# Four edits around the hand-over from MoE 1 to MoE 2: the queue that stores x's parts, the first part loads, the logits' steps and the Sinkhorn steps

## The chip, the cores and the metric

The kernel runs on one core of one Trainium2 chip. The metric is the device time of one execution in microseconds (us); lower is better. Three runs of the kernel before give a median of 2110.19 us (2109.23 to 2112.42).

## The reference, cut to what matters

```python
def reference(**kwargs):
    attn_out = _attn_ref(...)                    # B=4, H=8, S=576, D=64, causal attention plus a memory term
    x = attn_out.transpose(0, 2, 1, 3).reshape(2304, 512)
    x = (silu(x @ w_gate) * (x @ w_val)) @ w_out # MoE 1: 512 -> 1536 -> 512
    logits = x @ w_gate2                         # MoE 2: 8 experts, 512 -> 1024 -> 512
    P = np.exp(logits - logits.max())
    for _ in range(8):                           # Sinkhorn
        P /= P.sum(1, keepdims=True) + 1e-09
        P /= P.sum(0, keepdims=True) + 1e-09
        P *= N / E
    for e in range(E):
        out += P[:, e:e + 1] * (np.maximum(x @ w1[e], 0.0) @ w2[e])
```

## The kernel before, in words

Everything is computed in pairs of rounded halves: a value is cast to a high part, the rest is subtracted out as a low part, and three products (high by high, high by low, low by high) make one matrix product on TensorE. ScalarE (ACT) makes most of the casts, VectorE (DVE) most of the subtractions.

The tile framework fixes the order of each engine's instructions when the program is built, by a time model of its own; on the chip each engine takes its instructions strictly in that order. `keep_in_program_order` pins an instruction behind all that were traced before it on its engine; `issue_after(mark)` queues a block's instructions behind a mark on the mark's engine (in `behind`, the marks are the last load of a part, the last copy on ScalarE, and so on).

**x and its parts.** MoE 1 leaves x in one SBUF tile, `xacc`. MoE 2 uses a seven-product scheme on two by two blocks, so each pair of 256-token blocks of x is needed as seven parts (`B11`, `T1`, `T2`, `B21`, `T3`, `T4`, `B22`), each 512 KB as a pair of halves. `parts` (L731) and `parts_of` (L704) make them: a cast on ScalarE into a tile of `xl`, which has two buffers (L717); in the next step the subtraction on VectorE (L720); in the step after it a store to DRAM, issued on SyncE (SP, L723). The cast two parts later needs the same `xl` buffer, so it waits until that store has landed. Pairs 0 and 1 are made in MoE 1's third stage (14 stores), pair 2 in its last stage (7), pair 3 and the last 256 tokens in the first two pairs of MoE 2 (9): 30 stores. All loads of the kernel are issued on the same SP queue.

**MoE 2.** It goes over 16 units (half an expert each) and, in each, over four pairs of blocks and a rest. `unit_hidden` (L1257) makes a pair's hidden values in seven steps "H", of 12 matmuls each (L1270), every one with one part of x, read back from DRAM into a tile `xr` (four buffers, L1484). The function `right` keeps three part loads ahead of the one in use. The first four are issued before the loop, and their memory is that of the tiles of x that MoE 1's last matmuls "p" (L546) read. Chains of H steps sum into one PSUM bank `pc`, which ScalarE copies out between two of them (`keep`, L1277). Steps "O" make the output: `first_out` in unit 0 (L546, `pq`, copied to the sum by VectorE, L1410), `unit_out` after it (L1433, L1439). The output sum takes the memory of x, so L1410 cannot write before the last reader of x is done.

**Beside unit 0** run two generators, advanced by `behind` as the H and O steps go on: `last_parts` (every second step) and `routing` (every step). `routing` makes the logits of the last two chunks (`logits`, L672, with `two` set: tokens 1536 to 2047, m = 4, and 2048 to 2303, m = 2) and then the Sinkhorn iteration (`sinkhorn`, L1094). Each `yield` ends a step. The logits take 3 yields for each of 4 blocks and 2 more; in each block there is a cast (L681), a yield, a subtraction (L683), two yields and then the matmuls (L688). A Sinkhorn iteration takes five VectorE operations (L1112 to L1116), a yield, a matmul with ones (L1119), a yield and four VectorE operations (L1121 to L1124). The tiles `h` of the hidden values are in the pool `hc`, with eight buffers (`split_h`, L1242).

Of the kernel before, what the change touches and what calls it, by code (L numbers as in the profile page):

```python
# [9 lines left out]
F32R = mybir.dt.float32r  # L10
# [4 lines left out]
ALU = mybir.AluOpType  # L15
# [4 lines left out]
P = 128  # L20
B, H, S, D = 4, 8, 576, 64
NP = H // 2
NT = B * S
# [4 lines left out]
E = 8  # L28
# [104 lines left out]
def f32(ap):  # L133
    return ap.bitcast(F32)
# [21 lines left out]
def placed(pool, name, by):  # L156

    return pool.tile([P, 2 * 512 + 64], F32R, name=name)[:, by:by + 2 * 512].rearrange("p (a n) -> p a n", a=2)


class Kernel:
# [508 lines left out]
    def logits(self, psum, name, pool, first, last, two=None):  # L670

        nc, m = self.nc, last - first  # L672
        pl = psum.tile([P, 512], F32, name=name)
        for k in range(NK):
            src = self.x[:, k, first * P:last * P]
            if two:
                t = [pool.tile([P, 512], F32R, name=two)[:, 0:m * P] for _ in range(2)]
            else:
                t = pool.tile([P, 2, 512], F32R, name="xl")
                t = [t[:, a, 0:m * P] for a in range(2)]  # L680
            nc.scalar.copy(t[0], src)  # L681
            yield
            nc.vector.tensor_sub(t[1], src, f32(t[0]))  # L683
            yield
            if two:
                yield
            for a in range(2):
                nc.tensor.matmul(  # L688
                    pl[0:2 * E, 0:m * P], self.wgs[:, k], t[a], start=k + a == 0, stop=k == NK - 1 and a == 1
                )  # L690
        lt = pool.tile([P, 512], F32, name=two) if two else f32(pool.tile([P, 2, 512], F32R, name="xl")[:, 0])
        lt = lt[0:2 * E]
        nc.vector.tensor_copy(lt[:, 0:m * P], pl[0:2 * E, 0:m * P])
        yield
        yield
        pl = psum.tile([P, 512], F32, name=name)
        for t in range(m):
            nc.tensor.transpose(pl[:, t * 2 * E:(t + 1) * 2 * E], lt[:, t * P:(t + 1) * P], self.ident[0:2 * E, 0:2 * E])
        sums = self.Pw[:, first:last]
        pl = pl[:, 0:m * 2 * E].rearrange("p (t a e) -> p t a e", a=2, e=E)  # L700
        nc.vector.tensor_copy(sums, pl[:, :, 0])
        nc.vector.tensor_add(sums, sums, pl[:, :, 1])

    def parts_of(self, todo):  # L704


        nc, rest = self.nc, []
        for src, dst in [*todo, (None, None), (None, None)]:
            nxt = []
            for what in rest:  # L710
                nxt += what()
            rest = nxt
            if src is not None:
                src = src()
                t = self.xl.tile([P, 2, 512], F32R, name="xl")
                hi, lo = (t[:, n].rearrange("p (k t) -> p k t", k=2) for n in range(2))
                nc.scalar.copy(hi, src)  # L717

                def low(src=src, dst=dst, t=t, hi=hi, lo=lo):
                    nc.vector.tensor_sub(lo, src, f32(hi))  # L720

                    def store():
                        nc.sync.dma_start(dst, f32(t))  # L723
                        return []

                    return [store]

                rest.append(low)
            yield

    def parts(self, pair):  # L731

        t0, to = 2 * HT * pair, self.xparts[pair]
        q = {
            f"B{k + 1}{t + 1}": self.x[:, 2 * k:2 * k + 2, t0 + HT * t:t0 + HT * (t + 1)]
            for k in range(2) for t in range(2)
        }

        def total(name, a, b):
            def made():  # L740
                q[name] = self.tmpp.tile([P, 2, HT], F32, name="ws")
                self.nc.vector.tensor_sub(q[name], q[a], q[b])
                return q[name]

            return made

        plain = lambda name: lambda: q[name]
        yield from self.parts_of([
            (plain("B11"), to[0]), (total("T1", "B12", "B11"), to[3]), (total("T2", "B22", "T1"), to[2]),
            (plain("B21"), to[1]), (total("T3", "B22", "B12"), to[5]), (total("T4", "B21", "T2"), to[6]),  # L750
            (plain("B22"), to[4]),
        ])

    def moe1(self, last):

# [2 lines left out]
        with ExitStack() as st, ExitStack() as waiting, ExitStack() as banks:  # L758
# [61 lines left out]
            def more(c, logits):  # L820
                t0, n = CHUNKS1[c]
                if logits:
                    yield from self.logits(pgv, "p0", self.xl, t0 // P, (t0 + n) // P)
                yield from self.parts(c)

            gws = self.stream(lambda: self.gwp, [P, 2, 2, 512], "gw", self.keptg * 2, 2)
            wss = self.stream(lambda: wsp0, [P, 2, 512], "ws", self.kepto * 2, 3)
# [87 lines left out]
            def both():  # L915

                steps = iter(lambda: next(self.prep0), 2)

                def behind():
                    while True:  # L920
                        with ExitStack() as order:
                            for ins in self.last_half:
                                order.enter_context(tc.issue_after(ins.ins))
                            if next(steps, self) is self:
                                return
                        yield

                weights0 = behind()
                for c in (1, 2):
                    t0, n = CHUNKS1[c]  # L930
                    for _ in self.logits(plog, "pl", self.xl, t0 // P, (t0 + n) // P):
                        yield next(weights0, None)
                for _ in self.parts(2):
                    yield next(weights0, None)
                for _ in weights0:
                    yield
# [157 lines left out]
    def sinkhorn(self, pool, psum):  # L1094
        nc, Pw = self.nc, self.Pw
        mx = pool.tile([P, 1], F32, name="mx")
        nc.vector.tensor_reduce(mx, Pw, axis=AX.XY, op=ALU.max)
        yield
        pt = psum.tile([P, 512], F32, name="pu")
        nc.tensor.transpose(pt[0:1, 0:P], mx, self.ident)  # L1100
        m1 = pool.tile([1, 1], F32, name="m1")
        nc.vector.tensor_reduce(m1, pt[0:1, 0:P], axis=AX.X, op=ALU.max, negate=True)
        yield
        pt = psum.tile([P, 512], F32, name="pu")
        nc.tensor.matmul(pt[:, 0:1], self.ones[0:1, :], m1, start=True, stop=True)
        nm = pool.tile([P, 1], F32, name="nm")
        nc.vector.tensor_copy(nm, pt[:, 0:1])
        nc.scalar.activation(Pw, Pw, AF.Exp, bias=nm)
        r = pool.tile([P, NTT, 1], F32, name="r")
        cs = pool.tile([P, E], F32, name="cs")  # L1110
        for _ in range(8):
            nc.vector.tensor_reduce(r[:, :, 0], Pw, axis=AX.X, op=ALU.add)  # L1112
            nc.vector.tensor_scalar_add(r, r, 1e-9)
            nc.vector.reciprocal(r, r)
            nc.vector.tensor_mul(Pw, Pw, r.to_broadcast([P, NTT, E]))
            nc.vector.tensor_reduce(cs, Pw.rearrange("p t e -> p e t"), axis=AX.X, op=ALU.add)  # L1116
            yield
            pt = psum.tile([P, 512], F32, name="pu")
            nc.tensor.matmul(pt[:, 0:E], self.ones, cs, start=True, stop=True)  # L1119
            yield  # L1120
            nc.vector.tensor_scalar_add(cs, pt[:, 0:E], 1e-9)  # L1121
            nc.vector.reciprocal(cs, cs)
            nc.vector.tensor_scalar_mul(cs, cs, float(NT / E))
            nc.vector.tensor_mul(Pw, Pw, cs.unsqueeze(1).to_broadcast([P, NTT, E]))  # L1124


# [115 lines left out]
    def split_h(self, h, name, src, relu, n=512):  # L1242

        nc = self.nc
        t = self.hp.tile([P, 2, 512], F32R, name="h")[:, :, 0:n]
        shape = dict(j=2) if len(src.shape) == 3 else {}
        t2 = t.rearrange("p a (j n) -> p a j n", j=2)
        h[name] = t2
# [198 lines left out]
    def moe2(self):  # L1447
        nc, tc = self.nc, self.tc
        with ExitStack() as st:
# [9 lines left out]

            def last_parts():  # L1460

                yield from self.parts(PAIRS2 - 1)
                t0 = 2 * HT * PAIRS2
                yield from self.parts_of([
                    (lambda n=n: self.x[:, 2 * n:2 * n + 2, t0:NT], self.xparts[PAIRS2][n]) for n in range(2)
                ])

            def routing():
                for c in range(3, len(CHUNKS1)):
# [5 lines left out]
                      for i in ((0, 1, 2, 5, 3, 4, 6) if p < PAIRS2 else (0, 1))]  # L1475
            place, tiles = {x: n for n, x in enumerate(stream)}, []

            def right(u, p):
                def part(i):
                    n = place[u, p, i]  # L1480
                    while len(tiles) < min(n + 4, len(stream)):
                        _, q, k = stream[len(tiles)]
                        tiles.append(placed(xrp, "xr", 0 if k else 24))
                        self.marks[0] = nc.sync.dma_start(f32(tiles[-1]), self.xparts[q][k])  # L1484
                    return tiles[n]

                return part
# [124 lines left out]
```

## Time and profile before

| | |
|---|---|
| median of 3 runs | 2110.19 us (2109.23 to 2112.42) |
| the profiled execution, its own time | 2108.75 us |
| its span, first to last instruction | 2107.0 us |
| around the span | 1.75 us |
| TensorE (PE) busy | 2065.8 us, 98% of the span |
| VectorE (DVE) busy | 1718.9 us, 82% |
| ScalarE (ACT) busy | 974.1 us, 46% |
| GpSimd (POOL) busy | 523.0 us, 25% |
| mean granted TensorE clock | 0.998 of full speed |

The profile page comes from one execution. Its times are counted from the span's start. A line in a wait view reads: who waited, for whom, how many us in all, how often, the longest. In a timeline a row is a run of like instructions: start, length, engine, line, operation, and in square brackets how long the engine stood idle before it and what ended that. MoE 1's third stage, where the parts of pairs 0 and 1 are made, lies from 429 to 583 us, its last stage from 583 to 675 us, unit 0 of MoE 2 from 675 to about 795 us.

### The profile page before, as it was taken

What the parts mean: (1) busy time and instruction counts of PE and PEld (TensorE: products, weight loads), DVE (VectorE), ACT (ScalarE), POOL (GpSimd) and SP (SyncE); (2) the same over time, 40 slices, a digit from 0 to 9 for tenths busy, and PEclk for the clock granted to TensorE, in tenths of its full rate; (3) what the DMA queues carried; (4) which work ended last, traced back from release to release, by engine and by line L of the source; (5) the groups of instructions that cost most, each with busy time, mean ns of one, the idle gap of its engine ahead of it and who ended that gap; (6) DMA issues with size and microseconds to landing.
All of it is one profiled execution on the core that took longest, in us unless ns stands there. A gap on an engine that the chain in (4) does not pass through costs nothing.

```text
span 2107.0 us, 40598 instructions
## 1 busy us (share of the span) xinstructions
PE 2065.8 (98%) x15848; PEld 1904.7 (90%) x15848; DVE 1718.9 (82%) x3201; ACT 974.1 (46%) x1912; POOL 523.0 (25%) x458
## 2 busy tenths in 40 slices
PE   7999999999999999999999999999999999999999
PEld 5666787877889779999999999999999999999998
DVE  7899899674454578888888888988889888898887
ACT  7999543353333324444444444444444444444432
POOL 6888553000000032122121221212212122121210
PEclk9999999999999999999999999999999999999999
DMA  5342687375587837566475664755647556476564
GB/s 191 114 140 83 195 286 263 132 262 194 171 284 250 300 106 250 184 216 221 160 242 194 205 221 160 248 193 201 225 161 245 197 194 230 160 242 204 186 212 159
DMA packets 123359, 425.77 MB, mean 202 GB/s; under 512 B 13600, under 2 KB 13600, under 8 KB 120096
## 3 DMA queue, kind: packets, MB, share of 16 engines
q1 hardware_dynamic: 123168, 423.17, 59.9%
q8 instruction: 126, 2.06, 0.4%
q14 instruction: 65, 0.53, 0.1%
HBM read 374.36 MB, written 48.76 MB: 201 GB/s over the span
## 4 chain that ended last, share of the span: by engine, by line
PE 69%; DVE 11%; DMA 3%; issue 1%; ACT 1%; SPq 0%; DVEq 0%; ACTq 0%
PE pu L1433 16%; PE pc L1270 14%; PE pq L1433 11%; PE pt L1270 10%; PE po L546 5%; PE pt L1356 4%; PE p L546 3%; PE pc L546 3%; DVE m L1286 2%; DVE xacc L1439 2%; PE pt L546 2%; PE pq L546 2%; DMA xp<-xl 2%; DVE h L1255 1%; DVE h L1252 1%; DMA xr<-xp 1%
## 5 line engine op out<-in xcount | busy, mean ns | idle before, releaser
L1433 PE MATMUL pu<-xl,h 128*128 128x256 f32 x3240 | 424.8, 278 | 2.8 <-DVE xacc L1439 2.3
L1433 PEld LDWEIGHTS pu<-xl,h 128*128 128x128 f32 x3240 | 393.0, 188 | 7.2 <-DVE xacc L1439 4.0
L1270 PE MATMUL pc<-xr,w 128*128 128x256 f32 x3072 | 392.4, 277 | 4.9 <-DMA xr<-xp 3.4
L1270 PEld LDWEIGHTS pc<-xr,w 128*128 128x128 f32 x3072 | 369.1, 188 | 8.7 <-DMA xr<-xp 3.7
L1433 PE MATMUL pq<-xl,h 128*128 128x256 f32 x2430 | 316.9, 277 | 0.0
L1270 PE MATMUL pt<-xr,w 128*128 128x256 f32 x2304 | 294.1, 277 | 0.5 <-DMA xr<-xp 0.4
L1433 PEld LDWEIGHTS pq<-xl,h 128*128 128x128 f32 x2430 | 294.0, 188 | 0.3
L1254 ACT CAST h<-m 128x512 fp32r<-128x512 f32 (+1 forms) x345 | 190.3, 556 | 201.7 <-DVE m L1286 194.0
L1270 PEld LDWEIGHTS pt<-xr,w 128*128 128x128 f32 x2304 | 276.6, 188 | 1.8 <-issue 1.4
L1439 DVE SCALAR_TENSOR_TENSOR xacc<-pu,Pw,xacc 128x256 f32<-128x256 f32 x540 | 236.7, 474 | 38.7 <-PE pu L1433 38.6
L1277 ACT COPY m<-pc 128x512 f32<-128x512 f32 x192 | 112.1, 584 | 256.9 <-PE pc L1270 255.5
L1439 DVE SCALAR_TENSOR_TENSOR xacc<-pq,Pw,xacc 128x256 f32<-128x256 f32 x405 | 177.3, 473 | 47.1 <-PE pq L1433 47.1
L1255 DVE TENSOR_TENSOR h<-m,h 128x512 fp32r<-128x512 f32 (+1 forms) x345 | 207.0, 624 | 1.6
L1175 POOL TENSOR_TENSOR ws<-raw 128x512 f32<-128x512 f32 x60 | 80.8, 1358 | 502.7 <-DMA raw<-w 177.2
L1286 DVE SCALAR_TENSOR_TENSOR m<-m 128x512 f32<-128x512 f32 x240 | 187.0, 779 | 15.0 <-ACT m L1313 11.6
L1251 ACT ACTIVATE h<-m 128x512 fp32r<-128x512 f32 x192 | 121.4, 632 | 162.4 <-DVE m L1282 161.2
L1282 DVE TENSOR_TENSOR m<-pt,m 128x512 f32<-128x512 f32 x192 | 131.1, 683 | 57.5 <-ACT m L1277 51.4
L546 PE MATMUL p<-xs,gw 128*128 128x512 f32 (+1 forms) x864 | 171.0, 354 | 3.6 <-ACT hf L782 1.7
L546 PEld LDWEIGHTS p<-xs,gw 128*128 128x128 f32 x864 | 142.3, 188 | 30.7 <-DVE hf L783 2.8
L1252 DVE SCALAR_TENSOR_TENSOR h<-m,h 128x512 fp32r<-128x512 f32 x192 | 148.4, 773 | 7.6 <-ACT h L1251 7.2
L1162 POOL TENSOR_TENSOR w<-raw,w 128x512 fp32r<-128x512 f32 x15 | 38.6, 2574 | 435.3 <-ACT w L1161 435.3
L546 PE MATMUL po<-h,ws 128*128 128x512 f32 x576 | 144.6, 391 | 0.1
(229 smaller groups left out, 2943.0 us busy)
## 6 DMA issues: line engine op xcount, KB each, us to landing
xr<-xp SPq DMA_DIRECT2D x480, 512.0 KB, 4.1
raw<-w SPq DMA_DIRECT2D x64, 512.0 KB, 7.6
gw<-kg SPq DMA_DIRECT2D x24, 1024.0 KB, 7.1
graw<-gvo SPq DMA_DIRECT2D x36, 512.0 KB, 4.5
xp<-xl SPq DMA_DIRECT2D x30, 512.0 KB, 5.5
kg<-gw SPq DMA_DIRECT2D x24, 512.0 KB, 4.4
ws<-ko SPq DMA_DIRECT2D x24, 512.0 KB, 3.8
qk<-qkv SPq DMA_DIRECT2D x16, 640.0 KB, 4.9
```

The costliest lines, as they stand in the source:

```text
L546: self.nc.tensor.matmul(out, lhs[a], rhs[b], start=start and n == 0, stop=stop and n == 2, skip_group_check=shared)
L1251: nc.scalar.activation(hi, src, AF.Relu)
L1252: self.later(1, lambda: nc.vector.scalar_tensor_tensor(lo, src, 0.0, f32(hi), op0=ALU.max, op1=ALU.subtract))
L1254: nc.scalar.copy(hi, src)
L1255: self.later(1, lambda: nc.vector.tensor_sub(lo, src, f32(hi)))
L1270: self.marks[3] = nc.tensor.matmul(out[:, j * HT:(j + 1) * HT], w[:, a, j, k], x[:, b, k], start=start and j + k + n == 0, stop=k + n == 3 ...
L1277: self.marks[1] = nc.scalar.copy(t, src)
L1282: nc.vector.tensor_add(t, a, b)
L1286: relu = lambda out, a, b, op: nc.vector.scalar_tensor_tensor(out, a, 0.0, b, op0=ALU.max, op1=op)
L1356: nc.tensor.matmul(ph[:, j * HT:(j + 1) * HT], w[:, b, j, k], x[:, c, k], start=j + a + k + m == 0, stop=a + k + m == 4, skip_group_check= ...
L1433: nc.tensor.matmul(po[:, c], h[a][:, x, j, c * P:(c + 1) * P], w2[b][:, y, j], start=start and c + j + n == 0, stop=j + n == 3, skip_group ...
L1439: self.marks[2] = nc.vector.scalar_tensor_tensor(acc, po[:, c], self.Pw[:, at, e:e + 1], acc, op0=ALU.mult, op1=ALU.add)
```

## The change

All stores of parts are issued on ScalarE's queue in place of SP's. MoE 2's first seven part loads, in place of four, are issued before the loop: three go into tiles of `hc`, four into `xr`, each pinned behind what was traced before on SP; one tile of `hc` is set aside before them for the first hidden value. In the logits with `two` set, the cast and the subtraction stand in one step, and the second yield before the matmuls stays only for m = 4, so that the two chunks take 10 and 6 steps in place of 14 and 14. Each Sinkhorn iteration has one more yield before its matmul (three steps in place of two), and the factor NT/E is taken into the operation that adds 1e-9, so that one VectorE operation (L1123) falls away.

```diff
@@ logits @@
             nc.scalar.copy(t[0], src)
-            yield
+            if not two:
+                yield
             nc.vector.tensor_sub(t[1], src, f32(t[0]))
             yield
-            if two:
+            if two and m > 2:
                 yield
@@ parts_of, parts and their callers @@
-    def parts_of(self, todo):
+    def parts_of(self, todo, queue):
...
                     def store():
-                        nc.sync.dma_start(dst, f32(t))
+                        queue.dma_start(dst, f32(t))
...
-                yield from self.parts(c)
+                yield from self.parts(c, nc.scalar)
...
-                for _ in self.parts(2):
+                for _ in self.parts(2, nc.scalar):
...
-                yield from self.parts(PAIRS2 - 1)
+                yield from self.parts(PAIRS2 - 1, nc.scalar)
...
-                ])
+                ], nc.scalar)
@@ sinkhorn @@
             yield
+            yield
             pt = psum.tile([P, 512], F32, name="pu")
             nc.tensor.matmul(pt[:, 0:E], self.ones, cs, start=True, stop=True)
             yield
-            nc.vector.tensor_scalar_add(cs, pt[:, 0:E], 1e-9)
+            nc.vector.tensor_scalar(cs, pt[:, 0:E], 1e-9, float(E / NT), op0=ALU.add, op1=ALU.mult)
             nc.vector.reciprocal(cs, cs)
-            nc.vector.tensor_scalar_mul(cs, cs, float(NT / E))
@@ split_h @@
-        t = self.hp.tile([P, 2, 512], F32R, name="h")[:, :, 0:n]
+        t = (self.first_h.pop() if self.first_h else self.hp.tile([P, 2, 512], F32R, name="h"))[:, :, 0:n]
@@ moe2 @@
+            self.first_h = [self.hp.tile([P, 2, 512], F32R, name="h")]
+            ahead = [self.hp.tile([P, 2, 512], F32R, name="h") for _ in range(3)]
+
             def right(u, p):
                 def part(i):
                     n = place[u, p, i]
-                    while len(tiles) < min(n + 4, len(stream)):
+                    while len(tiles) < min(max(n + 4, 7), len(stream)):
                         _, q, k = stream[len(tiles)]
-                        tiles.append(placed(xrp, "xr", 0 if k else 24))
+                        tiles.append(ahead.pop() if ahead else placed(xrp, "xr", 0 if k else 24))
                         self.marks[0] = nc.sync.dma_start(f32(tiles[-1]), self.xparts[q][k])
+                        if len(tiles) < 8:
+                            tc.keep_in_program_order(self.marks[0])
                     return tiles[n]
```

## Rows read from the trace of the kernel before

**Rows 1.** The page, part 1: busy us, share of the span, instructions of each engine.
```profile
PE 2065.8 (98%) x15848; PEld 1904.7 (90%) x15848; DVE 1718.9 (82%) x3201; ACT 974.1 (46%) x1912; POOL 523.0 (25%) x458
```

**Rows 2.** Windows: stretch, length, busy us of each engine, TensorE clock, DMA share, GB/s.
```profile
425.00:490.00 65.00, 60.54 (x257) 48.01 (x256) 45.83 (x81) 29.52 (x48) 0.00 (x0) 0.97 0.74 255
...
668.00:735.00 67.00, 62.00 (x405) 53.27 (x405) 38.11 (x68) 24.53 (x45) 5.10 (x4) 1.00 0.82 290
735.00:780.00 45.00, 41.05 (x244) 34.43 (x243) 37.36 (x98) 10.55 (x19) 12.13 (x12) 1.00 0.29 94
...
860.00:2060.00 1200.00, 1198.56 (x10457) 1193.77 (x10456) 1048.18 (x1948) 525.91 (x931) 232.18 (x146) 1.00 0.61 205
```

**Rows 3.** Timeline of TensorE: three of its waits, in MoE 1 and in unit 0.
```profile
451.18 1.67 PE L546 MATMUL pc<-ws 128*128 128x512 f32 x6 [1.37 <-ACT hf L1062]
...
479.50 2.93 PE L546 MATMUL pc<-ws 128*128 128x512 f32 x6 [3.02 <-ACT hf L1062]
...
709.43 1.65 PE L1270 MATMUL pc<-xr,w 128*128 128x256 f32 x12 [2.55 <-DMA xr<-xp]
```

**Rows 4.** Timeline of ScalarE: casts that waited for a store to land.
```profile
450.03 0.62 ACT L717 CAST xl<-ws 128x512 fp32r<-128x512 f32 x1 [3.51 <-DMA xp<-xl]
...
478.35 0.62 ACT L681 CAST xl<-xacc 128x512 fp32r<-128x512 f32 x1 [6.05 <-DMA xp<-xl]
...
701.03 0.62 ACT L717 CAST xl<-xacc 128x512 fp32r<-128x512 f32 x1 [4.01 <-DMA xp<-xl]
```

**Rows 5.** Chain that ended last: stores from issue to landing (start, us).
```profile
443.47 6.53 DMA xp<-xl
451.39 3.31 DMA xp<-xl
...
468.29 10.04 DMA xp<-xl
```

**Rows 6.** Timeline of the SP queue: loads of gate weights issued just before two stores.
```profile
441.51 0.32 SPq L654 DMA_DIRECT2D gw<-kg  x1
...
467.09 0.32 SPq L654 DMA_DIRECT2D gw<-kg  x1
```

**Rows 7.** Windows, the two microseconds after the longer of MoE 1's waits.
```profile
481.00:483.00 2.00, 2.00 (x6) 1.60 (x5) 0.00 (x0) 0.96 (x2) 0.00 (x0) 0.52 0.01 2
```

**Rows 8.** Waits of TensorE from 665 to 830 us: who for whom, us, times, longest.
```profile
PE pu L1119 <- DVE cs L1116: 3.9, 5, 1.3
PE pc L1270 <- DMA xr<-xp: 3.4, 4, 2.5
...
PE pc L1270 <- ACT m L1277: 0.4, 1, 0.4
```

**Rows 9.** Waits of the SP queue from 640 to 900 us.
```profile
SPq L723 <- DVE xl L720: 14.1, 6, 4.2
SPq L1484 <- PE p L546: 12.9, 2, 12.6
```

**Rows 10.** DMA from 668 to 725 us: all that was moved, and the stores.
```profile
DMA packets 4898, 17.86 MB, mean 313 GB/s; under 512 B 544, under 2 KB 544, under 8 KB 4896
...
xp<-xl SPq DMA_DIRECT2D x9, 512.0 KB, 6.3
```

**Rows 11.** Timeline of the SP queue, 702 to 707 us: a store and the loads behind it.
```profile
702.40 0.32 SPq L723 DMA_DIRECT2D xp<-xl  x1
702.83 4.17 SPq L1484 DMA_DIRECT2D xr<-xp  x4
```

**Rows 12.** Timeline of VectorE: last read of x by the logits, first write of the sum.
```profile
713.17 0.41 DVE L683 TENSOR_TENSOR m<-xacc,m 128x256 fp32r<-128x256 f32 x1
713.62 1.29 DVE L1410 COPY xacc<-pq 128x512 f32<-128x512 f32 x2
```

**Rows 13.** Line L1119: count, ns least/median/most, first and last start.
```profile
L1119 PE MATMUL pu<-cs,ones x16: 256/266/277, 739.1 to 774.7; 128*128 128x8 f32 x16
```

**Rows 14.** Groups of VectorE, 730 to 778 us: busy us, mean ns, idle before.
```profile
L1123 DVE TENSOR_SCALAR cs<-cs 128x8 f32<-128x8 f32 x8 | 2.3, 286 | 0.2
```

More of the change, by code (lines that the diff above doesn't have):

```diff
@@ L729, in parts_of, with parts @@
             yield
-    def parts(self, pair):
+    def parts(self, pair, queue):
         t0, to = 2 * HT * pair, self.xparts[pair]
@@ L751, in parts @@
             (plain("B22"), to[4]),
-        ])
+        ], queue)
     def moe1(self, last):
@@ L1465, in last_parts @@
                     (lambda n=n: self.x[:, 2 * n:2 * n + 2, t0:NT], self.xparts[PAIRS2][n]) for n in range(2)
-                ])
+                ], nc.scalar)
             def routing():
```

## The prediction

> **What bounds the kernel now.** I read the page's engine shares first: TensorE is busy for 98% of the span, every other engine far less [rows 1]. The windows by stage then say where the missing time lies [rows 2]. From 860 to 2060 us TensorE works 1198.56 of 1200 us: the 15 units after unit 0 leave nothing to gain. Idle time that this change can reach lies in three stretches: 65.00 - 60.54 = 4.46 us where MoE 1 makes the parts of pairs 0 and 1, 67.00 - 62.00 = 5.00 us at the hand-over and in the first pairs of unit 0, and 45.00 - 41.05 = 3.95 us under the Sinkhorn iteration. So some 13 us are at stake. What ends the waits is in the wait views and timelines.
>
> In MoE 1 TensorE waits twice, 1.37 and 3.02 us, for ScalarE's copy of the bank pc [rows 3]. The copy was late because a cast in front of it on ScalarE stood 3.51 and 6.05 us for a store of parts to land [rows 4]. Those two stores took 6.53 and 10.04 us; one without a large load right ahead took 3.31 us [rows 5]. Ahead of both, on the same SP queue, a 1 MB load of gate weights had been issued 1.2 to 2 us before [rows 6]. After the longer wait the granted clock read 0.52, the lower of the two levels (1.2 GHz) after an idle stretch of 3 us [rows 7], and the same six matmuls took 2.93 in place of 1.67 us [rows 3].
>
> In unit 0 TensorE waits 3.4 us for loads of parts and 0.4 us for a copy of ScalarE, and 3.9 us in five waits for VectorE's column sums of the Sinkhorn iteration [rows 8]. The SP queue itself stood 14.1 us in six waits for VectorE's subtraction before a store could go, and its first part loads 12.6 us for matmuls "p" of MoE 1 [rows 9]. The DMA engines moved 17.86 MB in 57 us there [rows 10]. The longest wait of TensorE, 2.55 us, shows the blocking: a store was issued at 702.40, the moment its subtraction was done, and four loads went out behind it from 702.83 [rows 11]; TensorE got its part at 709.43 [rows 3].
>
> **Stores on ScalarE's queue: MoE 1's waits.** 30 issues leave SP and join ScalarE's stream. In MoE 1 the gain is the two waits and the slow matmuls: 1.37 + 3.02 + (2.93 - 1.67) = 5.65, say 5.7 us. It needs the first store to land within 6.53 - 1.37 = 5.2 us and the second within 7.0 us. No row shows a store from a second queue. The ends are 3.31 us, a store with no large load ahead, and today's 6.53 and 10.04 us. On its own queue a store has no load ahead of it, so I take the row 3.31 with room for sharing the engines, and count 5.7 us; the ends for the range are 0 and 5.7.
>
> That row shows a store being later when a 1 MB load is ahead in its queue. The Trainium skill, page "DMA: Bandwidth & Descriptors", section "Issuing engines are not separate DMA queues", says otherwise: transfers from any issuing engine run interleaved on the same 16 DMA engines, and a second issuer saves only issue time. By that rule this term would be near nothing.
>
> **Stores on ScalarE's queue: their cost.** An issue takes 0.32 us on SP [rows 11]; as long on ScalarE, 30 of them are 9.6 us of an engine that is busy for 29.5 of 65 and 24.5 of 67 us in these stretches [rows 2]. Besides, ScalarE now waits where SP did: the cast at 701.03 ended at 701.65 [rows 4] and its store went at 702.40 [rows 11], so 0.75 us for the subtraction alone, and 14.1 / 6 = 2.35 us when VectorE is behind [rows 9]. Queued behind the waiting store are the copies of pc, and TensorE waits for those. The order set at build time puts other ScalarE work between cast and store, so most of this should be covered by ScalarE's idle half. If a copy is late, the nearest row is the one late copy in unit 0, 0.4 us [rows 8]. Ends: 0, and 0.4 us for each of 30, 12 us. I charge six: 2.4 us.
>
> **Loads no longer blocked, and three of them early.** SP keeps only loads, so the loads at 702.83 need not wait for 702.40, and three of the seven first parts no longer move between 668 and 725 us. At 313 GB/s [rows 10] a part of 512 KB takes 1.7 us, so about 5 us of transfers leave the full stretch. They need buffers that are free earlier than those that waited for "p" [rows 9]; tiles of hc are another region. The gain is at most 3.4 + 0.4 = 3.8 us [rows 8], at least nothing. I take the 2.55 us wait whole and a third of the other 1.25: 3.0 us. What is late next is ScalarE's copy.
>
> **Logits in fewer steps.** 28 steps become 16, with the same instructions. VectorE now stands behind the cast of its own step; it is busy for 38 of 67 us there [rows 2], so I cost that at nothing; without that cover it would be at most a cast's 0.62 us [rows 4], eight times, on VectorE. The use: the sum cannot be written before x's last reader. That was the logits' subtraction at 713.17, and the first write followed at 713.62 [rows 12], so outputs can start earlier and give TensorE work while parts are on their way. This supports the 3.0 us above; I count nothing more.
>
> **Sinkhorn spaced.** Eight matmul pairs start from 739.1 to 774.7 us [rows 13]: 35.6 us for 7 iterations of two steps, so 2.5 us a step. TensorE's waits there are at most 1.3 us [rows 8]; one more step ahead of the matmul covers each. The dropped operation takes 8 x 0.286 = 2.3 us from VectorE [rows 14], off this very chain. Ends: 3.9 us, and nothing, if VectorE is later because the iteration now starts 12 steps earlier and runs beside the last parts. A loss is excluded only as long as the chain ends before unit 1 needs its weights, and 16 + 24 + 2 = 42 steps end before today's 46. I take three quarters: 2.9 us.
>
> **Sum.** 5.7 - 2.4 + 3.0 + 2.9 = 9.2 us. The profiled execution took 2108.75 us, 1.44 us under the median of 2110.19. 2108.75 - 9.2 = 2099.55; with the 1.44 the median should be 2101.0 us.
>
> **The rivals.** *The second queue separates nothing* (the same engines carry it all): MoE 1's casts wait as before. Against it stands the 3.31 us store, for it the DMA share of 0.74 and 0.82 in these stretches [rows 2]. Then -2.4 + 3.0 + 2.9 = 3.5 us, 2106.7. This is the skill's rule, section as above; the trace, with one queue only, cannot refute it. *ScalarE becomes the blocked queue* (slower): each store holds it for VectorE, as SP was held [rows 9], and TensorE waits for the copies behind. It eats the gains of 5.7 + 3.0 + 2.9 = 11.6 us from 11.6 / 30 = 0.39 us a store, and the kernel is measurably slower from (11.6 + 4.2) / 30 = 0.53 us. At 0.8 us, a third of SP's mean wait of 2.35: 24 - 11.6 = 12.4 us more, 2122.6. Against it: ScalarE's idle half. *The early loads are not early*: if the three tiles lie under tiles that are read until MoE 1's end, about 675 us, the pinned loads hold SP until then, the first part lands at best as long after as the store of 3.31 us took [rows 5], while unit 0 now begins at once, and the 3.0 turns into about -2.5: 5.7 - 2.4 - 2.5 + 2.9 = 3.7 us, 2106.5. *Transfers and VectorE stay the limit of unit 0* and give both gains there back: 5.7 - 2.4 = 3.3 us, 2106.9.
>
> **How the numbers follow.** A measurement of this kernel can tell about 0.2% from no change, 4.2 us: faster means under 2106.0, slower over 2114.4. Chances: my forecast 0.60, the queue that separates nothing 0.17, ScalarE blocked 0.10, loads not early 0.07, unit 0 still limited 0.06. The three middle cases lie within a microsecond of the border, so I give 0.08 of their 0.30 to faster: faster 0.68, same 0.22, slower 0.10. The range starts at the best ends, 5.7 + 3.8 + 3.9 = 13.4 us without cost, 2096.8, and 1.3 us of spread below it, 2095.5; it ends at 2109.5, past the three middle cases. ScalarE blocked stays outside.
>
> **What would show it.** Right: a second hardware queue with 30 stores, landing in 3 to 5 us; no ScalarE cast in MoE 1 waiting over 3 us; TensorE near 64 of 65 us from 425 to 490; three part loads issued before MoE 1's last "p" matmuls end; no wait over 1 us for a part; waits for the column sums under 1 us in all. Wrong: ScalarE idle for VectorE ahead of its issues, and TensorE waiting for copies of pc more than the 4.8 us it does now; or stores that still take over 6 us.

## The result, and the profile after

The changed kernel is slower. Its median is 2121.68 us (2118.27 to 2125.47, 6 runs) against 2109.54 us (6 runs) of the kernel before beside it: ratio 1.0057, 95% interval 1.0043 to 1.0072. The prediction was 2101.0 us, with 2109.5 as the upper end of its range. The profiled execution of the changed kernel took 2123.41 us, 2121.6 of them its span. (Lines from L683 on are one higher than before; the column sums' matmul in the Sinkhorn iteration is L1121, the part loads' line L1488.)

The page after: busy time of the engines, the DMA queues, and the stores of parts with their median time to landing.

```profile
PE 2073.3 (98%) x15848; PEld 1912.7 (90%) x15848; DVE 1719.0 (81%) x3193; ACT 973.7 (46%) x1912; POOL 524.2 (25%) x458
...
q1 hardware_dynamic: 118848, 407.44, 57.6%
q10 hardware_dynamic: 4320, 15.73, 1.9%
...
xp<-xl ACTq DMA_DIRECT2D x30, 512.0 KB, 5.5
```

The second queue is there with its 30 stores; its median of 5.5 us is the one that the page of before has for the same stores on SP. TensorE is busy 7.5 us longer than in [rows 1] for the same 15848 matmuls, so some of them ran slower.

Windows of the changed kernel, columns as in [rows 2]; the stretch from 583 us, MoE 1's last stage, was full in the kernel before, whose row for it stands first. In the changed kernel MoE 1 reaches into the stretch from 668 us, up to 691 us.

```profile
583.00:668.00 85.00, 85.00 (x572) 76.79 (x570) 41.11 (x76) 28.25 (x56) 0.00 (x0) 1.00 0.80 285
```

```profile
425.00:490.00 65.00, 54.85 (x226) 42.92 (x225) 41.01 (x71) 24.89 (x42) 0.00 (x0) 0.95 0.66 228
490.00:583.00 93.00, 93.00 (x407) 75.32 (x406) 45.97 (x79) 34.69 (x57) 0.79 (x1) 1.00 0.57 184
583.00:668.00 85.00, 81.80 (x504) 71.52 (x503) 40.17 (x75) 27.77 (x55) 0.74 (x1) 0.96 0.80 279
668.00:735.00 67.00, 59.34 (x397) 53.38 (x397) 35.36 (x68) 24.25 (x47) 0.00 (x0) 0.95 0.63 219
735.00:780.00 45.00, 45.00 (x277) 39.62 (x276) 37.11 (x87) 11.29 (x21) 10.67 (x8) 1.00 0.64 226
```

The loss is where the largest gain had been counted, in the two stretches of MoE 1 that make parts. Idle time there is 10.15 + 3.20 us, against 4.46 + 0 before. The lower clock costs about 65 x 0.05 + 85 x 0.04 = 6.7 us, against 65 x 0.03 = 2.0 before. Together that is about 13.6 us more. The last "pp" matmul (L546 into the bank pp, MoE 1's last output) starts at 689.4 us in place of 674.2: 15.2 us later, of which 1.4 was already there at MoE 1's third stage. Unit 0 gives 2.8 us back: from its first hidden matmul to unit 1's first output it takes 809.2 - 691.7 = 117.5 us, 795.6 - 675.3 = 120.3 before. The Sinkhorn stretch is full now, as predicted.

Timeline of TensorE in the changed kernel: its longest waits in MoE 1, which answer to [rows 3], and the first matmul of MoE 2.

```profile
455.89 2.93 PE L546 MATMUL pc<-xs,ws 128*128 128x512 f32 x6 [5.63 <-ACT hf L1063]
...
482.79 1.43 PE L546 MATMUL pc<-xs,gw 128*128 128x512 f32 x5 [2.43 <-ACT sg L1089]
...
653.24 5.79 PE L546 MATMUL po<-h,ws 128*128 128x512 f32 x12 [3.20 <-ACT h L803]
...
691.70 1.67 PE L1271 MATMUL pc<-h,w 128*128 128x256 f32 x12 [1.99 <-DVE ws L743]
```

TensorE waits for ScalarE, as before, only longer, and the six matmuls after the wait of 5.63 us take 2.93 us, as in [rows 3]. The window behind it shows the lower of the two clock levels (1.2 GHz), as [rows 7] did:

```profile
456.00:460.00 4.00, 4.00 (x10) 3.17 (x11) 0.52 (x1) 1.14 (x3) 0.00 (x0) 0.50 0.74 239
```

Timeline of ScalarE around two of these waits; they answer to [rows 4].

```profile
443.92 1.98 ACTq L724 DMA_DIRECT2D xp<-xl  x2
445.94 0.62 ACT L803 CAST h<-sg 128x512 fp32r<-128x512 f32 x1 [1.46 <-DVE xl L721]
...
452.41 0.62 ACT L718 CAST xl<-xacc 128x512 fp32r<-128x512 f32 x1 [5.37 <-DMA xp<-xl]
454.22 0.62 ACT L718 CAST xl<-ws 128x512 fp32r<-128x512 f32 x1 [1.19 <-DMA xp<-xl]
...
455.27 0.56 ACT L1063 COPY hf<-pc 128x512 f32<-128x512 f32 x1
...
650.82 0.62 ACT L718 CAST xl<-xacc 128x512 fp32r<-128x512 f32 x1 [5.23 <-DMA xp<-xl]
651.35 0.40 ACT L803 CAST h<-sg 128x256 fp32r<-128x256 f32 x1
```

Read it backwards: TensorE needs the copy at 455.27; ahead of it stand two casts of parts, and the first stood 5.37 us for a store to land, the second another 1.19. In [rows 4] one cast stood ahead of the copy, not two. The wait list of ScalarE from 420 to 735 us (who for whom, us, times, longest) shows what it stands for, first in the kernel before, then in the changed one:

```profile
ACT xl L717 <- DMA xp<-xl: 18.2, 12, 4.0
...
ACT xl L681 <- DMA xp<-xl: 6.7, 2, 6.1
```

```profile
ACT xl L718 <- DMA xp<-xl: 31.2, 13, 5.4
...
ACT xl L681 <- DMA xp<-xl: 3.8, 1, 3.8
...
ACT h L803 <- DVE xl L721: 1.5, 1, 1.5
ACT sg L783 <- DVE xl L721: 1.1, 1, 1.1
```

For landings it is 31.2 + 3.8 = 35.0 us, 18.2 + 6.7 = 24.9 before. For VectorE's subtraction ahead of an issue, the price of the rival "ScalarE becomes the blocked queue", it is 2.6 us in all.

The early loads: SP's waits from 640 to 900 us in the changed kernel, and TensorE's from 665 to 830 us, which answer to [rows 9] and [rows 8].

```profile
SPq L1488 <- PE pp L546: 20.5, 1, 20.5
```

```profile
PE pc L1271 <- DMA xr<-xp: 3.3, 2, 2.0
PE pc L1271 <- DVE ws L743: 2.0, 1, 2.0
PE pt L1271 <- DMA xr<-xp: 1.6, 1, 1.6
PE pc L1271 <- DMA h<-xp: 0.6, 1, 0.6
```

The loads are not early: the first of the seven stood 20.5 us for MoE 1's last "pp" matmuls, which read the tiles h and ws; in the built program its tile lies under ws, MoE 1's last output weights. The six others are pinned behind it. It landed at 691.56 us, 0.14 us before the first matmul of MoE 2, so the wait of 1.99 us there, which the profile puts down to VectorE, is likely the landing's: in the run of the loads alone, below, the same wait is put down to it. The waits for column sums are gone.

### The profile page after: what moved, and what is told of

It is laid out like the page before. It is cut to its first block, busy times and chain, and to the rows that moved or that the text cites. A ratio compares the mean times of both kernels' runs of the same rounds, so it can differ in the third digit from the quotient of the medians.

```text
span 2121.6 us, 40573 instructions
## 1 busy us (share of the span) xinstructions
PE 2073.3 (98%) x15848; PEld 1912.7 (90%) x15848; DVE 1719.0 (81%) x3193; ACT 973.7 (46%) x1912; POOL 524.2 (25%) x458
## 4 chain that ended last, share of the span: by engine, by line
PE 69%; DVE 10%; DMA 4%; ACT 1%; issue 1%; SPq 0%; ACTq 0%; DVEq 0%
PE pu L1434 15%; PE pc L1271 14%; PE pq L1434 10%; PE pt L1271 10%; PE po L546 5%; PE pt L1357 4%; PE pc L546 3%; PE p L546 2%; DVE m L1287 2%; PE pq L546 2%; DVE xacc L1440 2%; DMA xr<-xp 2%; PE pt L546 2%; DMA xp<-xl 2%; DVE h L1256 2%; DVE h L1253 1%
## 5 line engine op out<-in xcount | busy, mean ns | idle before, releaser
L546 PE MATMUL p<-xs,gw 128*128 128x512 f32 (+1 forms) x864 | 170.5, 354 | 2.9 <-ACT hf L783 1.2
L546 PEld LDWEIGHTS p<-xs,gw 128*128 128x128 f32 x864 | 142.4, 188 | 29.4 <-DVE hf L784 2.4
L546 PE MATMUL po<-h,ws 128*128 128x512 f32 x576 | 147.5, 399 | 3.2 <-ACT h L803 3.2
```

What stands on the lines that cost most here:

```text
L546: self.nc.tensor.matmul(out, lhs[a], rhs[b], start=start and n == 0, stop=stop and n == 2, skip_group_check=shared)
```

## The experiments

Each ratio is to the kernel before, run beside the version on the same chip (its medians lie between 2106.66 and 2109.23 us). It is taken over all runs and lies near the ratio of the means; where the runs of a version scatter, the ratio of the medians differs from it by up to some 0.1%. Hunks named @@ are those of the diff ahead of the prediction.

### Each part alone

Stores: the hunk @@ parts_of, parts and their callers @@, all else as before.

```diff
-                yield from self.parts(c)
+                yield from self.parts(c, nc.scalar)
```

> The kernel before with one part of the change: all 30 stores of x's parts issued on ScalarE's queue. Theory A (the stores on ScalarE are the loss): MoE 1 ends 10 to 14 us later than before, TensorE idles about 10 us between 425 and 490 us, and the kernel takes 2118 to 2124 us. Theory B (the loss is the first part load, which the change makes wait for MoE 1's last matmuls): this kernel has the old loads, so it is within 4 us of before or faster. Theory C (a second queue does shorten the stores, and the loss comes from the closer packed logits and Sinkhorn): a gain of about 5 us.

Measured: 2126.68 us, ratio 1.0089 (1.0072 to 1.0106): 18.8 us more. This part is the whole loss and more.

Loads: the hunks @@ split_h @@ and @@ moe2 @@.

```diff
-                    while len(tiles) < min(n + 4, len(stream)):
+                    while len(tiles) < min(max(n + 4, 7), len(stream)):
```

> The kernel before with the seven first part loads alone. Theory A: the first load waits for MoE 1's last matmuls and unit 0 starts 1 to 2 us later, a loss of 0 to 3 us in all. Theory B: all of the loss, 10 us or more, shows here. If the loads were early, as the change says, a gain of about 3 us.

Measured: 2106.19 us, ratio 0.9997 (0.9987 to 1.0006). The timeline of TensorE shows why nothing came of it: the wait of 2.55 us of [rows 3] became 1.62, and a new one stands before the first H step.

```profile
670.91 1.68 PE L1270 MATMUL pc<-h,w 128*128 128x256 f32 x12 [2.15 <-DMA h<-xp]
...
703.37 1.64 PE L1270 MATMUL pc<-xr,w 128*128 128x256 f32 x12 [1.62 <-DMA xr<-xp]
```

Logits: the hunk @@ logits @@.

```diff
-            if two:
+            if two and m > 2:
```

> The kernel before with the logits in 16 steps alone. Theories A and B: within 2 us of before, since the matmuls and casts are the same and x's last reader comes earlier by some us at most. Theory C: 3 us or more slower, since VectorE stands behind casts of its own step.

Measured: 2105.62 us, ratio 0.9987 (0.9978 to 0.9996).

Sinkhorn: the hunk @@ sinkhorn @@.

```diff
             yield
+            yield
```

> The kernel before with the spaced Sinkhorn iteration alone (one more step, one VectorE operation less in each). Theories A and B: TensorE's 3.9 us of waits for the column sums go, 2105 to 2107 us. Theory C: no gain, since the chain of VectorE stays as long.

Measured: 2102.89 us, ratio 0.9984 (0.9973 to 0.9994), with one wait for the column sums left, 1.7 us in place of 3.9 in five. With the logits alone one of 1.8 us is left; with both (the run of all but the stores below) none stands in the list. Added up, the three parts are worth 0.03 + 0.13 + 0.16 = 0.32%.

### All but the stores, and loads that are really early

```diff
             self.first_h = [self.hp.tile([P, 2, 512], F32R, name="h")]
+            tc.keep_in_program_order(nc.gpsimd.memset(f32(self.first_h[0][:, 0, 0:1]), 0.0))
```

A first use of `first_h` before the loads gives the first load other memory, freed earlier.

> The kernel before with the early loads, and a one-column memset that makes the first load's tile take memory freed at about 662 us, where in the kernel after it lay under MoE 1's last output weights (read to about 674 us before). Theory (the loads alone gave nothing because all seven were pinned behind that first one): the first three loads go out from 662 to 664 us, TensorE does not wait for the first part any more (2.15 us with the loads alone) and the time is 2102 to 2105 us, 2 to 4 under the kernel before's 2107.9. Rival (the loads' start decides nothing, the DMA engines and VectorE are the limit of unit 0): the loads go early, but the waits move to the fourth and later parts and the time stays at 2105 to 2108.

Measured: 2106.23 us, ratio 0.9996 (0.9987 to 1.0006). The loads go out early, as the timeline of SP shows:

```profile
657.66 1.27 SPq L1488 DMA_DIRECT2D h<-xp  x3
663.60 2.60 SPq L1488 DMA_DIRECT2D xr<-xp  x4
```

No wait for a part in unit 0 is over 1 us any more, and yet the time is the same. In the profiled execution, whose 2108.36 us are above the median, the gain was given back in the next units: from 860 to 1130 us TensorE was busy 266.28 of 270 us, against 269.81 before, with waits for loads such as

```profile
984.61 1.65 PE L1270 MATMUL pc<-xr,w 128*128 128x256 f32 x12 [1.46 <-DMA xr<-xp]
```

So the rival's time holds, and the start of these loads decides nothing by itself. That the waits move to the next units each time is not shown, since this is one execution.

The change with the stores on SP:

```diff
                     def store():
-                        queue.dma_start(dst, f32(t))
+                        nc.sync.dma_start(dst, f32(t))
```

> The kernel after with all stores back on SP and nothing else undone. Theory (the stores are the whole loss): 2100 to 2105 us, some 17 to 20 us under the kernel after's 2121.7 and 3 to 8 under the kernel before's. Rival (the parts hinder each other, the early loads hold SP's stores in unit 0): 2106 to 2112 us.

Measured: 2098.22 us, ratio 0.9958 (0.9944 to 0.9973). That is 0.42% under the kernel before, and the three parts' sum of 0.32% lies within its interval. Against it the changed kernel is 1.0057 / 0.9958 = 1.0% slower: the stores' price.

The same, and with the memset on `first_h` of the run of really early loads:

> Logits, Sinkhorn and the early loads with the freed tile, all stores still on SP. If the parts add up: -1.5 (logits), -3.5 (Sinkhorn), -2 to -4 (loads): 2099 to 2101 us, faster than both kernels. If the logits, the loads and the Sinkhorn steps compete for the same idle time of 735 to 780 us: 2102 to 2104 us.

Measured: 2097.15 us, ratio 0.996 (0.9947 to 0.9973). Both beat both kernels, and cannot be told from each other.

### Which side of the stores costs

```diff
-                yield from self.parts(c, nc.scalar)
+                yield from self.parts(c, nc.gpsimd)
```

> The kernel before with the 30 stores issued on GpSimd, which computes next to nothing until 735 us. Theory (ScalarE's own stream is the loss: stores and the two casts that wait for their landing stand ahead of copies of pc): a second queue alone costs nothing, 2104 to 2112 us, the waits in MoE 1 at most 5 us. Rival (any second queue makes stores land later behind the other queue's loads): stores still land in a median of 5.5 us or more and the time stays near 2127 us, as with the stores on ScalarE.

Measured: 2126.12 us, ratio 1.0092 (1.0077 to 1.0107). My theory fell: with no store in ScalarE's stream the loss is the same.

The opposite split, gate and output weights loaded on GpSimd's queue (L654), stores on SP:

```diff
-                self.nc.sync.dma_start(f32(tiles[-1]), sources[len(tiles) - 1])
+                self.nc.gpsimd.dma_start(f32(tiles[-1]), sources[len(tiles) - 1])
```

> The reverse split: all stores stay on SP, MoE 1's streamed gate-weight and output-weight loads (1 MB and 512 KB) go to GpSimd's queue. Theory (the splitting is the loss, whichever side moves): stores near a 1 MB load land in 8 to 10 us, and the time is 2115 to 2128 us. Rival (the issuer of the stores matters): 2104 to 2112 us.

Measured: 2121.94 us, ratio 1.0057 (1.004 to 1.0074). Whichever side moves, splitting costs.

Both on GpSimd's queue: the stores of parts, L654, and L899, L946 and L1025 in the same way.

```diff
-                    nc.sync.dma_start(self.kepth[f], s3)
+                    nc.gpsimd.dma_start(self.kepth[f], s3)
```

> As the run with the stores on GpSimd's queue, but MoE 1's gate-weight, output-weight, hidden-half and sum loads and its small stores go to GpSimd's queue too, so that stores and large loads share one queue again, only another one. Theory (the loss is the splitting: on one queue a store goes ahead of every load issued after it and a load waits behind a store, on two they share the engines and end together): stores near a 1 MB load land in 5 to 7 us instead of 8 to 9.6, TensorE is busy 60 to 64 of the 65 us from 425 to 490, and the time is 2105 to 2113 us. Rival (a store from any queue but SP's is slow, or the new order of ScalarE's instructions is the loss): 2120 to 2128 us.

Measured: 2110.77 us, ratio 1.0015 (1.0002 to 1.0028). One queue again, another one, and the loss is nearly gone.

Casts of the parts on GpSimd, stores on ScalarE:

```diff
-                nc.scalar.copy(hi, src)
+                nc.gpsimd.tensor_scalar(hi, src, 1.0, 1.0, op0=ALU.mult, op1=ALU.mult)
```

> Stores on ScalarE as in the kernel after, but the casts of the parts, which wait for the landing of the store two parts before, on GpSimd. Theory (late landings cost only because the cast that waits for them stands ahead of copies on ScalarE): stores still land in 8 to 9.6 us near the loads, TensorE's waits for ScalarE in MoE 1 are under 4 us in all instead of 10, MoE 1 ends within 3 us of the kernel before's and the time is 2104 to 2112 us, unless the casts on GpSimd, some 2 us each, hold VectorE. Rival (ScalarE's own waits for the subtraction, or the full DMA engines alone, are the loss): 2118 us or more.

Measured: 2127.31 us, ratio 1.0085 (1.0068 to 1.0102). I had looked for the loss to go. It moved: VectorE's subtraction now stands for the late cast, ahead of the low part that TensorE waits 5.60 us for. Timeline of VectorE:

```profile
648.49 0.69 DVE L720 TENSOR_TENSOR xl<-ws,xl 128x512 fp32r<-128x512 f32 x1 [5.49 <-POOL xl L717]
649.10 0.68 DVE L803 TENSOR_TENSOR h<-h,h 128x512 fp32r<-128x512 f32 x1
```

Only the nine stores of MoE 2 on ScalarE:

```diff
-                yield from self.parts(PAIRS2 - 1)
+                yield from self.parts(PAIRS2 - 1, nc.scalar)
```

> Only MoE 2's nine stores on ScalarE, MoE 1's 21 on SP. Theory (the loss is made in MoE 1, next to the 1 MB loads, and in unit 0 the split helps or does nothing): 2103 to 2109 us, within 0.2% of the kernel before. Rival (the loss follows the number of stores, 0.6 us each): 2111 to 2114 us.

Measured: 2110.38 us, ratio 1.0013 (1.0 to 1.0027), so nearly all of the loss belongs to MoE 1's 21 stores.

### Landing or order

The built programs differ in one more thing. As soon as stores and loads stand on different queues, the build puts casts of parts further ahead in ScalarE's stream (and VectorE's subtractions with them). With all on GpSimd's queue ScalarE's order is that of the kernel before but for one instruction, so that run could not tell the two apart. Whether the transfers or this order cost was still open. Edges that fix the order without a wait take them apart: from MoE 1's third stage on, to its end, each instruction of ScalarE, VectorE and TensorE is put behind the one that precedes it in the other build. The order on SP and GpSimd is left to the build. In the traces the three engines' instructions of MoE 1 then stand in the order meant, from 420 us on.

```diff
     with tile.TileContext(nc) as tc:
         body(tc, *args)
+        in_order(tc)
...
+def in_order(tc):
...
+    for chain in STREAMS:
+        names = [f"I-{n}" for n in chain.split()]
+        for a, b in zip(names, names[1:]):
+            tc.add_manual_dep(by[b], a, no, reason="in_order")
```

> Stores on GpSimd's queue, but through all of MoE 1 the instructions of ScalarE, VectorE and TensorE are kept in the order that they have in the kernel before. If the order is the loss: 2104 to 2111 us, MoE 1's waits as in the kernel before. If the late landing by itself is the loss: 2118 to 2127 us, and the wait of 5.4 us at about 649 us stays. If each is half: about 2115 us.

> All stores on SP as in the kernel before, but through all of MoE 1 the three engines keep the order that they have with the stores on GpSimd's queue. If the order is the loss: 2118 to 2127 us, with waits over 3 us at about 452, 470 and 649 us. If the late landing is the loss: 2104 to 2112 us.

> Stores on ScalarE's queue as in the kernel after, MoE 1 in the order of the kernel before; only the stores' own places in ScalarE's stream are new. If the order is the loss: at most 4 us over the kernel before for 30 issues and their waits, 2107 to 2113 us. If the late landing is: 2118 to 2130 us.

| stores' queue | order of before | order of the split build |
|---|---|---|
| SP, with the loads | 1 (the kernel before) | 1.0047 (1.0032 to 1.0062), 2118.53 us |
| GpSimd | 1.0047 (1.0032 to 1.0063), 2116.64 us | 1.0092 (1.0077 to 1.0107), 2126.12 us |
| ScalarE | 1.0092 (1.0066 to 1.0118), 2128.98 us | 1.0089 (1.0072 to 1.0106), 2126.68 us |

In the last row the order of the split build is the one of the stores alone, which is not in every place that of GpSimd's build.

With the stores on GpSimd the two causes are about half each, and they add up: 0.47 + 0.47 = 0.94 against 0.92%. By the medians it is 7.4 and 9.3 us against 19.5, so "half" holds no closer than the intervals. The two also lie in different stages (busy time of TensorE and clock):

| run | third stage, 425 to 490 us | last stage, 583 to 668 us |
|---|---|---|
| two queues, old order | 57.75 us at 0.95 | 85.00 us at 1.00 |
| one queue, new order | 60.53 us at 1.00 | 80.43 us at 0.98 |
| two queues, new order | 57.86 us at 0.95 | 79.57 us at 0.96 |

So the late landing costs in the third stage, the order mostly in the last. The full last stage of the first row also shows no cost of the edges there; a run with the edges alone, on one queue in the old order, was not made.

The same cast of MoE 1's last stage shows both. First ScalarE with one queue and the new order, where the longest time of a store to landing in MoE 1 was 7.5 us:

```profile
637.07 0.62 ACT L717 CAST xl<-xacc 128x512 fp32r<-128x512 f32 x1 [3.40 <-DMA xp<-xl]
637.59 0.40 ACT L802 CAST h<-sg 128x256 fp32r<-128x256 f32 x1
643.41 0.62 ACT L717 CAST xl<-ws 128x512 fp32r<-128x512 f32 x1 [5.41 <-DMA xp<-xl]
643.93 0.61 ACT L802 CAST h<-h 128x512 fp32r<-128x512 f32 x1
```

Then with two queues and the old order, where the store for which the last of these casts waits took 9.45 us in the trace:

```profile
640.75 0.62 ACT L717 CAST xl<-xacc 128x512 fp32r<-128x512 f32 x1 [0.69 <-DMA xp<-xl]
641.28 0.61 ACT L802 CAST h<-h 128x512 fp32r<-128x512 f32 x1
...
646.62 0.41 ACT L802 CAST h<-sg 128x256 fp32r<-128x256 f32 x1 [2.34 <-PE po L546]
647.82 0.62 ACT L717 CAST xl<-ws 128x512 fp32r<-128x512 f32 x1 [0.79 <-DMA xp<-xl]
```

In the new order the cast stands ahead of casts of "h" that TensorE needs, and an ordinary landing holds them 5.41 us; TensorE waited 4.35 us at 644.60. In the old order two casts of "h" go first, and even the late landing cost 0.79 us here. The third stage has the price of late landings. Timeline of TensorE, two queues and old order:

```profile
468.49 2.93 PE L546 MATMUL pc<-ws 128*128 128x512 f32 x6 [4.39 <-ACT hf L1062]
```

On ScalarE's own queue the old order does not help. There the store itself stands in the stream, behind VectorE and ahead of the copy, and a 7.64 us wait for a landing follows two issues. ScalarE's timeline and two of its waits (415 to 675 us), stores on ScalarE in the old order:

```profile
442.78 0.33 ACTq L723 DMA_DIRECT2D xp<-xl  x1
443.25 0.58 ACT L1062 COPY hf<-pc 128x512 f32<-128x512 f32 x1
444.49 0.33 ACTq L723 DMA_DIRECT2D xp<-xl  x1
451.46 0.62 ACT L717 CAST xl<-xacc 128x512 fp32r<-128x512 f32 x1 [7.64 <-DMA xp<-xl]
```

```profile
ACT xl L717 <- DMA xp<-xl: 18.0, 6, 7.6
...
ACT hf L1062 <- DVE xl L720: 5.3, 3, 2.2
```

The last row, copies held by a store that waits for VectorE, is the rival's mechanism, at 5.3 us. How the 0.92% splits on ScalarE was not taken apart further.

Not every store lands later on its own queue. The median of MoE 1's 21 stores is even lower, 4.2 us in the changed kernel and 4.0 with the stores on GpSimd against 5.4 before; the late ones stand beside a 1 MB load. With the stores on GpSimd, one was issued at 457.61 us, 0.29 us after a 1 MB load on SP at 457.32; the load landed at 466.62 and the store, half its size, at 466.80, 9.2 us after its issue. On one queue the store at 460.81 of the kernel before, 2.4 us behind a 1 MB load, took 6.02 us. In MoE 1, 4 of 21 stores took over 8 us with the stores on GpSimd or on ScalarE alone, 3 in the changed kernel, 2 to 6 in the other runs that split the queues there, and each of these late ones had a 1 MB load in flight beside it; with stores and loads on one queue none did in any trace, bar the one of 10.04 us in [rows 5].

Single packets show why, in the run of the stores alone. There a store was issued on ScalarE at 441.16 us beside a 1 MB load on SP at 441.17; they landed at 449.37 and 449.14. The DMA queues from 444 to 447 us (packets, MB, share of 16 engines; q1 has SP's loads, q10 the stores):

```profile
q1 hardware_dynamic: 90, 0.70, 62.3%
q10 hardware_dynamic: 96, 0.39, 31.9%
```

The two queues move packets in about equal numbers, but the load's are of about 8 KB and the store's of 4 KB. So the load gets nearly twice the bytes, and a store of half its size lasts as long as it does.

The Trainium skill, page "DMA: Bandwidth & Descriptors", section "Queues, rings and completion order", says that an engine takes packets in turn from the queues that have work. The trace agrees, with 90 and 96 packets in 3 us.

With the stores on GpSimd something is added that no run explains: from 458 to 462 us, with the store of 457.61 already issued, only SP's queue moved packets.

## Why the prediction was wrong

**Stores, MoE 1's waits: +5.7 us predicted, a loss measured.** This is the step that failed: "On its own queue a store has no load ahead of it, so I take the row 3.31", with ends of 0 and 5.7. A queue of its own is no path of its own. The row of 3.31 us, issued at 451.39, had no 1 MB load in flight: the one before it had landed at 448.68, the next went out at 458.42. So it was no price for a store beside a load; with the stores alone on ScalarE four took 8.2 to 9.7 us, each beside one. And the lower end left out a loss without a reason. Besides, the term was too large from the start: in the runs of the loads, the logits and the Sinkhorn steps alone, where MoE 1 is not touched, TensorE is busy 62.56 to 63.55 of the 65 us, in place of 60.54 in [rows 2]. The wait of 3.02 us behind a landing of 10.04 is in that one execution only; idle time of 1.5 to 2.4 us was all that there was to gain.

**Stores, cost on ScalarE: 2.4 us.** Its working took for granted that "the order set at build time puts other ScalarE work between cast and store". The order itself changed with the queue, and by itself it cost 0.47%. No row of before could show that; the change of order is a consequence of the edit that I didn't look for. The whole of the stores was +18.8 us alone, where I had 5.7 - 2.4 = 3.3 us of gain.

**Loads: 3.0 us predicted, 0.03% (-0.06 to 0.13%) measured.** The rival "the early loads are not early" came true to its mechanism: a tile under weights that are read to MoE 1's end. Its price, a wait at the start of unit 0, was 2.15 us alone. But loads that were early gave nothing alone either. That was in the rival "Transfers and VectorE stay the limit of unit 0", which however took Sinkhorn's gain away with it, and that gain came.

**Logits: nothing predicted, 0.13% measured.** TensorE's waits from 665 to 830 us fell from 9.0 to 7.1 us in its trace, those for column sums from 3.9 to 1.8 and those for parts from 3.8 to 1.1, and new ones of 1.6 and 1.1 us for VectorE came. So the cover held in the main, and the term had left out what fewer steps do to the waits of the Sinkhorn iteration behind them.

**Sinkhorn: 2.9 us predicted, 0.16% of 2107.89 = 3.4 us measured (1.3 to 5.7).** Right in mechanism and, within this interval, in size, though alone it left one wait of 1.7 us.

**The rivals.** "The second queue separates nothing" was right about the median of all 30 landing times, 5.5 us both ways. The rule of the Trainium skill that the prediction named for it, page and section as there, leaves a second issuer nothing but saved issue time. The runs do not agree: with the old order kept, the other queue by itself cost 0.47%. Neither the rival nor the rule gives the loss. "ScalarE becomes the blocked queue" had the sign, and its 2122.6 us lay near the 2121.68 measured by luck, for a mechanism that accounts for 2.6 us of ScalarE's waits; the same loss came without ScalarE. Its chance of 0.10 was low because I took ScalarE's idle half as cover: an idle half on the whole does not help the one copy that stands behind a cast.

## What to carry to other kernels

A second DMA queue did not take the stores out of the loads' way here; before a store moves, look for who waits for its landing, and price it from a row in which the same neighbours are moving. Where a build fixes the order of instructions, an edit to a queue can reorder engines that it does not name: compare the order of the streams first, then the trace. And a term that rests on one long wait of one execution should be read against a second execution.

## What was not expected of the hardware

A 512 KB store issued 0.29 us after a 1 MB load from another queue landed 0.18 us after it, in 9.2 us, though the shortest of that run's stores in MoE 1 took 2.9 us. Beside each other, two queues moved 90 and 96 packets in 3 us, and the one with packets of 8 KB got nearly twice the bytes. Seven loads that went out earlier, the first three by 10 us (657.66 against 667.38 us) and the four others by 5 (663.60 against 668.75), left the time of the kernel where it was.
